# Delta-rule attention with an MLP on one core: a pair of chunks solved in whole blocks of 32, the accumulators' copies put ahead of two activations, pieces of the first pair moved

## The chip, the cores and the metric

The kernel runs on one core of a Trainium2 chip. A core has engines that run side by side, each with its own in-order queue: TensorE (PE, matmuls from SBUF into PSUM), VectorE (DVE), ScalarE (ACT), GpSimd (POOL) and SyncE (SP), which here only issues transfers (DMA). The metric is the device time of one execution in microseconds (us). Before the change it is 641.29 us, the median of 3 runs (641.17 to 642.59).

## The reference, cut to what matters

Four batches, 8 heads, 768 time steps, head size 48. Each head runs a delta rule over time, and the result, 3072 tokens of 384 features, goes through an MLP with 2048 hidden units.

```python
k_n = k / (norm(k) + 1e-06)
for t in range(768):
    y[t] = q[t] @ state
    v_old = k_n[t] @ state
    state = state + beta[t] * outer(k_n[t], v[t] - v_old)
h = y @ w_in
g = where(h >= 1, h, where(h <= -1, 0, (h + 1) ** 2 / 4))
out = g @ w_out
```

## The kernel before, in words

**Chunks.** Time is cut into 12 chunks of 64 steps, taken in 6 pairs. Within a chunk the recursion is replaced by a triangular system: keys against keys (gram_k, L193), the inverse of a unit triangular matrix of size 64 for each head and batch, and products with values, queries and the state. The state lies in SU. For one chunk g the pieces on PE are gram_k, gram_q (L206, queries against keys), chain_r (L390, the state's part is taken from the values), chain_u (L405), chain_y (L419, the output of the attention) and chain_d (L465, the state's update).

**The triangular inverse.** lanes (L253) copies the blocks of 32 on the diagonal, transposes them so that each of 128 lanes of DVE holds one block, and works out the norms of the keys, N, and the factor gm from beta. Then there are two ways:

- In halves (G < WHOLE): the two blocks of 16 of each block of 32 are inverted by solve (L293), 15 steps of a product and a subtraction on DVE. unlanes (L326) puts them back. merge16_a and merge16_b (L340, L352) join two blocks of 16 into one of 32 by matmuls on PE, once for each of the two chunks; their results are subtracted and transposed again on DVE (L361, L362).
- Whole (G >= WHOLE): lanes scales the block (L280), POOL cuts the triangle (L281, affine_select) and sets the diagonal, and solve_whole (L304) inverts the block of 32 in 30 steps (L310 product, L312 addition). unlanes_whole (L315) scales, transposes back, and makes the transposed copies (L318, L320, L323).

In both ways merge32 (L366) joins blocks of 32 into 64 on PE. WHOLE is 2 before the change: the first two pairs go in halves, the other four whole. (G in lanes counts pairs of chunks.)

**The MLP and its slots.** The main loop (L738) walks over 104 items. An item is one block of 128 hidden units for one pair of chunks, and the pairs are the stages G = 0 to 5. Stage 0 has 24 items, of which the first 8 and the last 8 cover only one chunk (256 columns), and the others have 16 items of 512 columns. For an item n, PE does up (L605, 9 matmuls into the accumulator "h", 2 buffers); ACT and DVE work out g from it in place (L735 twice, L754, then the max with h, L762); in the next item ACT and DVE split it in two parts, ghi and glo (L730, L731); and down (L614) of that item follows two items later (LAG), into four accumulators o0 to o3 that stay open for a stage. When the last block of a chunk is through, store (L628) copies the accumulators out, those with even number on ACT, those with odd number on DVE (L631), and sends them off over SP.

**How the attention is fitted in.** Each item has two half slots. plan(G) (L649) writes by hand which attention piece runs in which half slot while stage G of the MLP runs: at(pe, G, t, ...) puts a piece on PE at item t of the stage, at(fill, G, t, ...) steps of DVE work or loads. Slot t of an integer comes after up and before down of the item, and its results are moved out within the item; slot t + 0.5 comes after down, and its results are moved out at the start of the next item. During stage 0 the chunks 2 and 3 are made ready, during stage 1 the chunks 4 and 5, and so on; the first up of stage G + 1 needs the chain_y of its second chunk, whose rows are partly sent through SP (L460). All these PE pieces share two PSUM accumulators, named "ch": a piece can start only when the piece that held its accumulator before has been moved out.

In stage 0 DVE and ACT also unpack the MLP's weights, which arrive as 64-bit numbers (weight, L163; run(wu, ...) in the loop).

Of the kernel before, what the change touches and what calls it, by code (L numbers as in the profile page):

```python
# [23 lines left out]
SMALL = 20  # L24
SOON = 8
PASSES = ((0, 0), (0, 1), (1, 0))
WHOLE = 2
LAG = 2


# [1 line left out]
def delta_rule_moe(ctx: ExitStack, tc: tile.TileContext, kqa, kqb, kv, beta, w, out):  # L32
# [220 lines left out]
    def lanes(G):  # L253

        A = S["A"] = sb.tile([P, 32, 32], F32, name="A", bufs=1)
        if G < WHOLE:
            X = S["X"] = sb.tile([P, 2, 16, 16], F32, name="X", bufs=1)
            Xf = X.rearrange("l s c t -> l (s c t)")
            nc.gpsimd.memset(X, 0.0)
            for s in range(2):  # L260
                nc.gpsimd.memset(Xf[:, 256 * s:256 * s + 256:17], 1.0)
            nc.gpsimd.memset(ZT[:, :, :, 16:32], 0.0)
        for g in range(2):
            for r in (0, C):
                (nc.scalar.copy if G else nc.vector.tensor_copy)(out=GG[r:r + 32, g, :, 32:64], in_=GG[r:r + 32, g, :, 0:32])
            yield
        nc.vector.transpose(out=A, in_=GG[:, :, :, 32:64].rearrange("p g u t -> p t (g u)"))  # L267
        yield
        n = sb.tile([P, 32], F32, name="N2")
        nc.vector.tensor_copy(out=n, in_=A.rearrange("l j t -> l (j t)")[:, 0:1024:33])  # L270
        r = norms(n)
        N = S["N"] = sb.tile([P, 32], F32, name="N3")
        nc.vector.transpose(out=N, in_=n)
        gm = S["gm"] = sb.tile([P, 32], F32, name="gm")
        nc.vector.reciprocal(out=r, in_=n)
        nc.vector.tensor_tensor(out=gm, in0=r, in1=beta_sb[:, G, :], op=ALU.mult)
        nc.vector.tensor_tensor(out=gm, in0=gm, in1=r, op=ALU.mult)
        yield
        if G >= WHOLE:
            nc.vector.scalar_tensor_tensor(out=A, in0=A, scalar=-1.0, in1=gm[:, :, None].broadcast_to([P, 32, 32]), op0=ALU.mult, op1=ALU.mult)  # L280
            nc.gpsimd.affine_select(out=A, in_=A, pattern=[[-1, 32], [1, 32]], base=0, channel_multiplier=0,  # L281
                                    compare_op=ALU.is_gt, fill=0.0)
            nc.gpsimd.memset(A.rearrange("l c t -> l (c t)")[:, 0:1024:33], 1.0)
            return
        A16 = S["A16"] = sb.tile([P, 2, 16, 16], F32, name="A16", bufs=1)
        for s in range(2):
            b = slice(16 * s, 16 * s + 16)
            nc.vector.tensor_tensor(out=A16[:, s], in0=A[:, b, b], in1=gm[:, b, None].broadcast_to([P, 16, 16]), op=ALU.mult)
        X32 = S["X32"] = sb.tile([P, 32, 32], F32, name="A", bufs=1)
        nc.gpsimd.memset(X32, 0.0)  # L290
        yield

    def solve():  # L293

        X, A16 = S["X"], S["A16"]
        for j in range(15):
            n, m = j + 1, 15 - j
            pr = sb.tile([P, 240], F32, name="pr", bufs=1)[:, 0:2 * n * m].rearrange("l (s c t) -> l s c t", s=2, t=m)
            nc.vector.tensor_tensor(out=pr, in0=X[:, :, 0:n, j:j + 1].broadcast_to([P, 2, n, m]),
                                    in1=A16[:, :, j:j + 1, j + 1:16].broadcast_to([P, 2, n, m]), op=ALU.mult)  # L300
            nc.vector.tensor_tensor(out=X[:, :, 0:n, j + 1:16], in0=X[:, :, 0:n, j + 1:16], in1=pr, op=ALU.subtract)
            yield
# [23 lines left out]
    def unlanes():  # L326

        X, X32, gm = S["X"], S["X32"], S["gm"]
        for s in range(2):
            b = slice(16 * s, 16 * s + 16)  # L330
            nc.vector.tensor_tensor(out=X32[:, b, b], in0=X[:, s], in1=gm[:, None, b].broadcast_to([P, 16, 16]), op=ALU.mult)
        yield
        nc.vector.transpose(out=XT[:, :, :, 32:64].rearrange("p g u t -> p t (g u)"), in_=X32.rearrange("l c t -> l t c"))
        yield
        nc.vector.transpose(out=ZT[:, :, :, 0:16].rearrange("p g u c -> p c (g u)"), in_=X32[:, 0:16, :])
        yield
# [160 lines left out]
    def products(*pieces):  # L497
        return [p() for p in pieces]
# [145 lines left out]
    def chain(G, t, a):  # L644
        for j, f, g in ((0, chain_u, a), (0.5, chain_y, a), (1.5, chain_d, a), (2.5, chain_r, a + 1), (3.5, chain_u, a + 1), (4, chain_y, a + 1), (5, chain_d, a + 1)):
            if (f, g) != (chain_d, ntot - 1):
                at(pe, G, t + j, lambda f=f, g=g: f(g))

    def plan(G):  # L649

        a, b = 2 * G + 2, 2 * G + 3
        if G == NS - 1:
            return
        va, vb = scale_v(a), scale_v(b)
        if G == 0:
            ln, so, un = lanes(1), solve(), unlanes()
            at(pe, G, 0, lambda: chain_y(1))
            at(fill, G, 0.5, (load_q, 3))
            at(pe, G, 0.5, lambda: chain_d(1))
            at(pe, G, 1, lambda: place_beta(1, NS))  # L660
            at(fill, G, 1, (load_kv, 3))
            at(pe, G, 1.5, lambda: gram_k(a))
            at(pe, G, 2.5, lambda: gram_k(b))
            lane_steps(G, 7, ln)
            for j in range(8):
                at(fill, G, 9.5 + j / 2, (so, 2))
            at(pe, G, 11.5, lambda: gram_q(a))
            at(pe, G, 12.5, lambda: gram_q(b))
            at(fill, G, 13.5, (un, 1))
            at(fill, G, 13.5, (un, 9))  # L670
            for j in range(2):
                at(fill, G, 10 + j, (va, 1))
                at(fill, G, 16 + j, (vb, 1))
            at(pe, G, 13.5, lambda: chain_r(a))
            M = 14
            for j, f in enumerate((merge16_a, merge16_b)):
                for g in range(2):
                    at(pe, G, M + j + g / 2, lambda f=f, g=g: f(g))
            M = 16
            last = 24  # L680
        else:
            so, un = solves.pop(G)
            at(fill, G, 0.5, (va, 1))
            at(fill, G, 1, (va, 1))
            at(pe, G, 2.5, lambda: chain_r(a))
            at(pe, G, 4.5, lambda: gram_q(a))
            at(pe, G, 6, lambda: gram_q(b))
            cost, hs = 0, 0
            for j in range(1, 31):
                at(fill, G, (-0.5 if G == 1 else -1.5) + hs / 2, (so, 1))  # L690
                cost += j * (31 - j) + 150
                hs = int(cost / 9461 * (15 if G == 1 else 17))
            for j, t in enumerate((7, 7.5, 8, 8)):
                at(fill, G, t, (un, 1))
            at(fill, G, 9, (vb, 1))
            at(fill, G, 9.5, (vb, 1))
            M = 8.5
            last = 16
        for j, x in ((0, (0, None)), (0.5, (1, 0)), (2.5, (None, 1))):
            at(pe, G, M + j, lambda x=x: merge32(*x))  # L700
        chain(G, M + 1.5, a)
        if G < NS - 2:
            at(fill, G, 6.5 if G else 14, (load_k, a + 2))
            at(fill, G, M + 0.5, (load_k, b + 2, (nc.sync, nc.sync), True))
            at(pe, G, M + 1, lambda: gram_k(a + 2))
            at(pe, G, M + 3.5, lambda: gram_k(b + 2))
            lane_steps(G, M + 2, lanes(G + 2), 2.5, 3, 3.5, 4)
            solves[G + 1] = solve_whole(), unlanes_whole()
            at(fill, G, M + 3, (load_q, a + 2))
            at(fill, G, M + 5, (load_k, b + 2))  # L710
            at(fill, G, M + 6.5, (load_q, b + 2))
            at(fill, G, last + 0.5, (load_kv, a + 2))
            at(fill, G, last + 1.5, (load_kv, b + 2))
# [24 lines left out]
    for n, item in enumerate(items):  # L738
        at_, c = 2 * n, cols(item[2])
        finish(late)  # L740
        if last:
            rest(*last)
            ready.append(last[0])
        h = up(*item)

        s = sb.tile([P, 2 * NB], F32, name="s", bufs=2)
        relu(s[:, c], h[:, c], mid, -0.5)
        evicts = products(*pe.pop(at_, []))
        run(wu, 3 if n < 3 else 1)
        fills(at_)  # L750
        finish(evicts)
        run(wu, 1)
        relu(s[:, c], s[:, c], one, -1.0)
        nc.scalar.activation(out=s[:, c], in_=s[:, c], func=AF.Square)  # L754
        if len(ready) == LAG:
            x = ready.pop(0)
            down(*x)
            for b in x[2]:
                if left[x[0], b] == 0:
                    store(x[0], b)  # L760
        late = products(*pe.pop(at_ + 1, []))
        nc.vector.tensor_tensor(out=s[:, c], in0=h[:, c], in1=s[:, c], op=ALU.max)  # L762
        run(wu, 2)
        fills(at_ + 1)
        last = item, s
# [53 lines left out]
```

## Time and profile before

| | |
|---|---|
| median of 3 runs | 641.29 us |
| the profiled execution | 640.05 us |
| its span, first to last instruction | 638.3 us |
| PE busy | 596.0 us (93%) |
| DVE busy | 413.8 us (65%) |
| ACT busy | 389.9 us (61%) |
| POOL busy | 29.7 us (5%) |
| mean granted PE clock | 0.954 |

How to read the rows. A row of the grouped view gives the line of the kernel, the engine, the operation, what it writes and reads, the shape and the count; after the first bar the busy time of the group and the mean duration of one in ns; after the second bar the time that the engine idled just before them, and what ended that. A row of the timeline has the start, the duration, the engine and line, the operation, and in brackets the idle time before it with its releaser. In the view by stretches each engine has its busy time and, in brackets, its count of instructions. PE counts each fp32 matmul of a piece twice. An engine's busy time can be the time in which several small matmuls overlap. Items can be told by up: the nine matmuls of L610.

### The profile page before, as it was taken

To read this page: it belongs to the slowest core of one execution; us is meant where nothing else is said; L and a number is where in the kernel's file an instruction comes from. 1 tells how busy PE (TensorE), PEld (TensorE's weight loads), DVE (VectorE), ACT (ScalarE), POOL (GpSimd) and SP (SyncE) were. 2 spreads that over 40 slices of the span, in tenths; PEclk is the share of its full clock that TensorE was granted. 3 is DMA by queue.
4 is the path that set the end of the run, shared out by engine and by line. 5 is a ranking of instruction groups with operands and counts; after the bars stand their busy time and mean duration, and the time that the engine had idled before them with its cause. 6 is when DMAs were issued, how large, how long until landed. Compare 5 with 4: busy or idle time off the path is not lost.

```text
span 638.3 us, 21794 instructions
## 1 busy us (share of the span) xinstructions
PE 596.0 (93%) x9584; PEld 514.9 (81%) x9584; DVE 413.8 (65%) x862; ACT 389.9 (61%) x679; POOL 29.7 (5%) x62
## 2 busy tenths in 40 slices
PE   8977777898898899999999999999999999999996
PEld 7657676687887787888888888888888888899995
DVE  3869789894257895458993469973389954343332
ACT  4126477753875558775569665568646586566663
POOL 2003000000002000002000010000020000000000
PEclk8685579999999999999999999999999999999999
DMA  5933483002032411113401114310214100010002
GB/s 170 370 94 107 143 269 94 2 4 56 17 81 51 114 29 30 37 35 90 110 18 30 43 39 116 91 28 7 66 48 110 35 2 15 4 44 18 0 1 50
DMA packets 32431, 42.54 MB, mean 67 GB/s; under 512 B 7056, under 2 KB 27152, under 8 KB 32336
## 3 DMA queue, kind: packets, MB, share of 16 engines
q1 hardware_dynamic: 31200, 39.00, 21.5%
q10 hardware_dynamic: 880, 2.07, 1.0%
q8 instruction: 75, 1.23, 0.8%
q14 instruction: 20, 0.16, 0.1%
q0 software_dynamic: 256, 0.08, 0.1%
HBM read 34.05 MB, written 4.72 MB: 61 GB/s over the span
## 4 chain that ended last, share of the span: by engine, by line
PE 57%; DVE 21%; ACT 10%; issue 6%; DMA 3%; SPq 2%; POOL 1%; DVEq 0%; ACTq 0%
PE o L625 20%; PE h L610 18%; PE ch L553 4%; PE ch L430 3%; DVE glo L731 3%; DVE pr L310 3%; DVE A L312 2%; DVE s L762 2%; ACT s L735 2%; ACT GG L385 2%; PE ch L395 2%; ACT XT L387 2%; PE ch L375 2%; DVE SU L487 1%; DVE A L267 1%
## 5 line engine op out<-in xcount | busy, mean ns | idle before, releaser
L610 PE MATMUL h<-xb,wt 128*128 128x512 f32 (+1 forms) x936 | 226.1, 387 | 8.5 <-DVE s L762 5.8
L625 PE MATMUL o<-wt,ghi 128*128 128x384 f32 x768 | 200.9, 343 | 3.9 <-DVE wx L631 3.0
L610 PEld LDWEIGHTS h<-xb,wt 128*128 128x128 f32 x936 | 165.4, 191 | 41.6 <-DVE s L762 7.8
L625 PEld LDWEIGHTS o<-wt,ghi 128*128 128x128 f32 x768 | 137.2, 189 | 12.9 <-DVE wx L631 4.3
L762 DVE TENSOR_TENSOR s<-h,s 128x512 f32<-128x512 f32 (+1 forms) x104 | 66.9, 644 | 114.9 <-ACT s L754 114.8
L625 PE MATMUL o<-wt,glo 128*128 128x384 f32 x384 | 130.3, 339 | 0.6 <-DVE glo L731 0.5
L730 ACT CAST ghi<-s 128x512 fp32r<-128x512 f32 (+1 forms) x104 | 61.2, 589 | 106.7 <-DVE s L762 95.2
L735 ACT ACTIVATE s<-h,half 128x512 f32<-128x512 f32 (+1 forms) x104 | 68.0, 654 | 49.4 <-PE h L610 49.1
L731 DVE TENSOR_TENSOR glo<-s,ghi 128x512 fp32r<-128x512 f32 (+1 forms) x104 | 66.9, 643 | 43.3 <-ACT ghi L730 43.3
L625 PEld LDWEIGHTS o<-wt,glo 128*128 128x128 f32 x384 | 72.4, 189 | 2.3 <-DVE glo L731 2.3
L735 ACT ACTIVATE s<-s,one 128x512 f32<-128x512 f32 (+1 forms) x104 | 72.1, 693 | 2.6
L754 ACT ACTIVATE s<-s 128x512 f32<-128x512 f32 (+1 forms) x104 | 62.3, 599 | 3.3
L310 DVE TENSOR_TENSOR pr<-A 128x30 f32<-128x30 f32 (+14 forms) x120 | 39.3, 328 | 6.4 <-POOL A L281 4.5
L312 DVE TENSOR_TENSOR A<-A,pr 128x30 f32<-128x30 f32 (+14 forms) x120 | 39.8, 332 | 4.4
L430 PEld LDWEIGHTS ch<-Q,SU 64*64 64x64 f32 (+3 forms) x1056 | 23.7, 141 | 4.5 <-ACT ghi L730 1.5
L430 PE MATMUL ch<-Q,SU 64*64 64x64 f32 (+3 forms) x1056 | 26.0, 228 | 0.6 <-ACT SU L415 0.6
L553 PE MATMUL ch<-SU 128*128 128x64 f32 (+1 forms) x72 | 24.0, 521 | 0.0
L553 PEld LDWEIGHTS ch<-SU 128*128 128x128 f32 x72 | 15.2, 279 | 8.1 <-issue 8.0
L456 DVE TENSOR_TENSOR xb<-ch,xb 128x384 fp32r<-128x384 f32 x22 | 12.1, 551 | 14.5 <-ACT X L451 10.2
L226 DVE TENSOR_TENSOR Q<-ch,mask 64x512 f32<-64x512 f32 (+1 forms) x30 | 20.6, 687 | 0.4
L281 POOL TENSOR_SCALAR_AFFINE_SELECT A<-A 128x1024 f32<-128x1024 f32 x4 | 5.1, 1264 | 299.5 <-DMA xb<-X 261.1
L487 DVE TENSOR_TENSOR SU<-ch,SU 48x384 f32<-48x384 f32 (+1 forms) x30 | 16.6, 555 | 0.7 <-PE ch L472 0.3
(129 smaller groups left out, 605.7 us busy)
## 6 DMA issues: line engine op xcount, KB each, us to landing
wt<-in_w_dram SPq DMA_DIRECT2D x14, 768.0 KB, 7.4
out_dram<-wx SPq DMA_DIRECT2D x47, 96.0 KB, 2.2
KV<-in_kv_dram SPq DMA_DIRECT2D x36, 96.0 KB, 2.4
KV<-in_kv_dram SPq DMA_DIRECT2D x72, 48.0 KB, 2.3
KV<-in_kv_dram SPq DMA_DIRECT2D x12, 192.0 KB, 2.8
xb<-X SPq DMA_DIRECT2D x66, 32.0 KB, 2.1
K<-in_kqb_dram SPq DMA_DIRECT2D x12, 128.0 KB, 2.7
Q<-in_kqb_dram SPq DMA_DIRECT2D x12, 128.0 KB, 2.7
```

The lines of the kernel that those rows point to most:

```text
L310: nc.vector.tensor_tensor(out=pr, in0=A[:, 0:n, j:j + 1].broadcast_to([P, n, m]), in1=A[:, j:j + 1, j + 1:32].broadcast_to([P, n, m]), op= ...
L312: nc.vector.tensor_tensor(out=A[:, 0:n, j + 1:32], in0=A[:, 0:n, j + 1:32], in1=pr, op=ALU.add)
L430: nc.tensor.matmul(yy[i][o * C:o * C + C, e, p], SF[rows, u:u + C], w_[rows, x, k, :], **how)
L487: nc.vector.tensor_tensor(out=x, in0=y, in1=x, op=ALU.add)
L553: nc.tensor.matmul(idle[:, 0:m], SF[:, 0:P], SF[:, 0:m], start=True, stop=True)
L610: nc.tensor.matmul(h[:, cols(bs)], WT[f][:, 0, x, k * P:(k + 1) * P], XB[G][:, y, k, cols(bs)], start=(n == 0), stop=(n == 8))
L625: nc.tensor.matmul(oacc[G, k], (ghi, glo)[x][:, k * P:(k + 1) * P], WT[f][:, 1, y, :], start=(new and n == 0), stop=(left[G, b] == 0 and n ...
L730: nc.scalar.copy(out=ghi[:, c], in_=s[:, c])
L731: nc.vector.tensor_tensor(out=glo[:, c], in0=s[:, c], in1=ghi[:, c], op=ALU.subtract)
L735: nc.scalar.activation(out=out, in_=in_, func=AF.Relu, bias=bias, scale=scale)
L754: nc.scalar.activation(out=s[:, c], in_=s[:, c], func=AF.Square)
L762: nc.vector.tensor_tensor(out=s[:, c], in0=h[:, c], in1=s[:, c], op=ALU.max)
```

## The change

- **The second pair is inverted whole.** WHOLE goes from 2 to 1, and plan(0) uses solve_whole and unlanes_whole. The four merges of 16 leave PE. The steps are spread by a function that was a loop in plan before, over twelve half slots from item 9.
- **Other slots in stage 0.** chain_d(1) goes from 0.5 to 1, the placing of beta from 1 to 4, the key Grams from 1.5 and 2.5 to 2 and 3, the query Grams from 11.5 and 12.5 to 13 and 16, chain_r(2) from 13.5 to 14, the steps of unlanes from 13.5 to 15 to 16, the scaling of the second chunk's values from 16 and 17 to 17.5 and 18.5, the loads of values and keys half an item later. merge32, the chain and what hangs on them (M) move from 16 to 16.5.
- **The accumulators' copies.** In the loop, down and store now stand ahead of the second and third activation of the item. On PE nothing changes by that; on ACT the copies of store come before these activations.

```diff
-WHOLE = 2
+WHOLE = 1
...
+    def spread(G, t, n, so):
+        cost, hs = 0, 0
+        for j in range(1, 31):
+            at(fill, G, t + hs / 2, (so, 1))
+            cost += j * (31 - j) + 150
+            hs = int(cost / 9461 * n)
...
-            ln, so, un = lanes(1), solve(), unlanes()
+            ln, so, un = lanes(1), solve_whole(), unlanes_whole()
             at(pe, G, 0, lambda: chain_y(1))
             at(fill, G, 0.5, (load_q, 3))
-            at(pe, G, 0.5, lambda: chain_d(1))
-            at(pe, G, 1, lambda: place_beta(1, NS))
-            at(fill, G, 1, (load_kv, 3))
-            at(pe, G, 1.5, lambda: gram_k(a))
-            at(pe, G, 2.5, lambda: gram_k(b))
+            at(pe, G, 1, lambda: chain_d(1))
+            at(fill, G, 1.5, (load_kv, 3))
+            at(pe, G, 2, lambda: gram_k(a))
+            at(pe, G, 3, lambda: gram_k(b))
+            at(pe, G, 4, lambda: place_beta(1, NS))
             lane_steps(G, 7, ln)
-            for j in range(8):
-                at(fill, G, 9.5 + j / 2, (so, 2))
-            at(pe, G, 11.5, lambda: gram_q(a))
-            at(pe, G, 12.5, lambda: gram_q(b))
-            at(fill, G, 13.5, (un, 1))
-            at(fill, G, 13.5, (un, 9))
+            spread(G, 9, 12, so)
+            at(pe, G, 13, lambda: gram_q(a))
+            at(pe, G, 16, lambda: gram_q(b))
+            for t in (15, 15.5, 16, 16):
+                at(fill, G, t, (un, 1))
             for j in range(2):
                 at(fill, G, 10 + j, (va, 1))
-                at(fill, G, 16 + j, (vb, 1))
-            at(pe, G, 13.5, lambda: chain_r(a))
-            M = 14
-            for j, f in enumerate((merge16_a, merge16_b)):
-                for g in range(2):
-                    at(pe, G, M + j + g / 2, lambda f=f, g=g: f(g))
-            M = 16
+                at(fill, G, 17.5 + j, (vb, 1))
+            at(pe, G, 14, lambda: chain_r(a))
+            M = 16.5
...
-            at(fill, G, 6.5 if G else 14, (load_k, a + 2))
+            at(fill, G, 6.5 if G else 14.5, (load_k, a + 2))
...
-        relu(s[:, c], s[:, c], one, -1.0)
-        nc.scalar.activation(out=s[:, c], in_=s[:, c], func=AF.Square)
         if len(ready) == LAG:
             x = ready.pop(0)
             down(*x)
             for b in x[2]:
                 if left[x[0], b] == 0:
                     store(x[0], b)
+        relu(s[:, c], s[:, c], one, -1.0)
+        nc.scalar.activation(out=s[:, c], in_=s[:, c], func=AF.Square)
```

More of the change, by code (lines that the diff above doesn't have):

```diff
@@ L687, in plan @@
             at(pe, G, 6, lambda: gram_q(b))
[L688 to L692, printed above, removed]
+            spread(G, *((-0.5, 15) if G == 1 else (-1.5, 17)), so)
             for j, t in enumerate((7, 7.5, 8, 8)):
```

## The prediction

> **What bounds the kernel now.** I read the page first, then the busy time by stretches, then the timelines of TensorE (PE), VectorE (DVE) and the DMA issue queue (SP) through the first stage.
>
> ```profile
> span 638.3 us, 21794 instructions
> PE 596.0 (93%) x9584; PEld 514.9 (81%) x9584; DVE 413.8 (65%) x862; ACT 389.9 (61%) x679; POOL 29.7 (5%) x62
> ...
> PEclk8685579999999999999999999999999999999999
> ```
>
> Over the span PE is the bound. But the edit lies in the first stage (G=0, about 75 to 202 us), and there the stretches say something else:
>
> ```profile
> core 0: us, PE busy (x) PEld busy (x) DVE busy (x) ACT busy (x) POOL busy (x), PEclk, DMA share, GB/s
> 81.90:114.60 32.70, 25.25 (x302) 21.55 (x303) 32.41 (x52) 25.96 (x52) 0.00 (x0) 0.90 0.54 154
> 119.80:147.60 27.80, 24.46 (x403) 20.75 (x406) 26.38 (x69) 14.45 (x23) 0.96 (x1) 1.00 0.06 17
> 147.60:166.10 18.50, 17.52 (x663) 15.33 (x651) 5.67 (x11) 8.99 (x16) 2.08 (x4) 1.00 0.10 27
> 166.10:193.70 27.60, 26.08 (x722) 23.37 (x722) 11.41 (x25) 22.05 (x48) 0.00 (x0) 1.00 0.22 56
> ```
>
> From 81.9 to 114.6 DVE is busy 32.41 of 32.70 us (weight unpacking) and PE has 7.4 us free. From 119.8 to 147.6 DVE is busy 26.38 of 27.80 (the lane steps and the solve of the second pair). Only from 147.6 to 166.1 does DVE have room, 12.8 us, and there PE is full (17.52 of 18.50): that is where the four merges of 16 stand. So the stage is bound by DVE until 147 us and by PE from there. The question is what happens if DVE gets about as much work as that room holds.
>
> **The change, part by part. 1: D, beta and the key Grams.**
>
> ```profile
> 82.79 0.29 PE L472 MATMUL ch<-SU,KV 64*48 64x48 f32 x4 [1.62 <-DVE A L457]
> 89.42 1.16 PE L199 MATMUL ch<-K 48*64 48x64 f32 x62 [1.44 <-ACT beta_sb L135]
> ...
> 108.71 1.33 PE L610 MATMUL h<-xb,wt 128*128 128x256 f32 x9 [1.23 <-DVE s L762]
> ```
>
> Both waits come from pieces that follow each other into the two "ch" accumulators: chain_d(1) waits 1.62 us for those of chain_y(1), gram_k(2) waits 1.44 us for that of the beta placing. Moved apart, both waits can go, 3.1 us. But DVE is full behind them, and its instructions there are the same ones. PE then waits for DVE longer at the following items, as it does already in the third row (1.23 us). I take 0: the cover is the DVE queue. The bounds are a gain of 3.1 (DVE not the limit after all) and a loss of about 1 (ACT now waits inside the item for the Grams, and the weight casts queue behind that). The key and value loads that are issued half an item later keep their order on SP.
>
> **2: the solve.** This is the term that decides.
>
> ```profile
> L312 DVE TENSOR_TENSOR A<-A,pr 128x30 f32<-128x30 f32 (+14 forms) x120 | 39.8, 332 | 4.4
> L310 DVE TENSOR_TENSOR pr<-A 128x30 f32<-128x30 f32 (+14 forms) x120 | 39.3, 328 | 6.4 <-POOL A L281 4.5
> ...
> L301 DVE TENSOR_TENSOR X<-X,pr 128x30 f32<-128x30 f32 (+7 forms) x30 | 7.6, 255 | 1.0
> L299 DVE TENSOR_TENSOR pr<-X,A 128x30 f32<-128x30 f32 (+7 forms) x30 | 7.6, 252 | 0.8
> ...
> L323 DVE STREAM_TRANSPOSE GG<-XT 128x512 f32<-128x512 f32 x8 | 5.2, 685 | 0.0
> ...
> L318 DVE TENSOR_TENSOR A<-A,gm 128x1024 f32<-128x1024 f32 x4 | 4.9, 1217 | 0.0
> ...
> L362 DVE STREAM_TRANSPOSE GG<-XT 128x512 f32<-128x512 f32 x4 | 2.8, 711 | 0.1
> ...
> L335 DVE STREAM_TRANSPOSE XT<-A 128x512 f32<-128x512 f32 x2 | 2.0, 998 | 0.0
> ...
> L331 DVE TENSOR_TENSOR A<-X,gm 128x256 f32<-128x256 f32 x4 | 1.5, 420 | 0.1
> ...
> L361 DVE TENSOR_TENSOR XT<-XT,ch 128x256 f32<-128x256 f32 x2 | 0.8, 420 | 4.1 <-PE ch L356 4.1
> ```
>
> Thirty steps over whole blocks cost (39.3 + 39.8)/4 = 19.8 us of DVE in each later stage, fifteen over halves (7.6 + 7.6)/2 = 7.6: +12.2. The final scaling becomes one instruction of 1024 elements for two of 256, 1.22 - 0.84 = +0.4; the first scaling, in the same shapes, +0.4 again. The first step now waits for the triangle that POOL cuts: 4.5 us over 3 stages in the L310 row, so +1.5 of idle DVE, since nothing stands between the two here. One transpose goes (-1.0), two of 512 columns come (+1.4), the subtractions and transposes of the merges go (-0.8, -1.4). Sum: **+12.7 us on DVE**, nearly all of it ahead of the room at 147.6.
>
> Between 119.8 (max(8)) and 166.1 (end of max(16)) DVE has 26.4 + 5.7 = 32.1 us of work, so it gets 44.8 in 46.3. The full stretch holds 1.4 us of gaps in 27.8; left at that the sum is 46.2, carried over in proportion 47.2. Half a microsecond of value scaling leaves the stretch. So max(16) ends between 165.5 and 166.6: I take 166.1, the time of before, only that DVE now arrives there without a pause. The up-products keep step with it, each waiting for the "h" buffer that the max two items earlier frees.
>
> **3: what PE saves, and what it waits for.**
>
> ```profile
> L344 PE MATMUL ch<-XT,GG 32*32 32x16 f32 x256 | 2.7, 180 | 2.3 <-DVE KV L401 2.2
> ...
> L356 PE MATMUL ch<-A,XT 32*32 32x16 f32 x256 | 2.9, 180 | 0.2 <-issue 0.2
> ```
>
> ```profile
> 164.41 0.21 PE L373 MATMUL ch<-XT,GG 32*32 32x32 f32 x1
> ...
> 166.00 1.34 PE L610 MATMUL h<-xb,wt 128*128 128x256 f32 x9
> ...
> 178.12 1.20 PE L375 MATMUL ch<-GG 32*32 32x32 f32 x64 [0.37 <-DVE X L457]
> ...
> 165.70 0.42 DVE L762 TENSOR_TENSOR s<-h,s 128x256 f32<-128x256 f32 x1 [4.30 <-ACT s L754]
> L226 DVE TENSOR_TENSOR Q<-ch,mask 64x512 f32<-64x512 f32 (+1 forms) x30 | 20.6, 687 | 0.4
> ```
>
> PE is spared 2.7 + 2.9 = 5.6 us of merges and the 2.3 us waited ahead of them. It can't cash them in before 166, because DVE leads. Then the new order bites: merge32 of the first group needs a "ch" accumulator, gram_q(3) now stands directly ahead of it and holds both, and the masks that empty them (three of 0.69) lie on DVE behind the transposes of the solve, just ahead of max(16). Their first accumulator comes free one mask and one half-width max before the end: 166.1 - 0.7 - 0.4 = 165.0. Before, PE had at 166.0 both merge32 pieces done.
>
> Left for PE until the last chain_y of the stage ends: the work of 166.1 to 193.7 (26.1 us), one merge32 (1.2), the double one (164.41 to 166.00, 1.6) and one up of 256 columns that now stands ahead of chain_y(3) (1.3): 30.2 us. Its waits were 27.6 - 26.1 = 1.5; with Grams and merges closer together on two accumulators I put them at 3.0, twice that, with 1.5 and 4.5 as ends. 165.0 + 33.2 = 198.2 against 193.7: **+4.5**.
>
> **4: the border to the next stage.**
>
> ```profile
> 174.27 2.24 PE L430 MATMUL ch<-Q,SU 112*64 112x64 f32 x96
> 191.48 2.24 PE L430 MATMUL ch<-Q,SU 112*64 112x64 f32 x96
> 201.86 2.34 PE L610 MATMUL h<-xb,wt 128*128 128x512 f32 x9 [1.26 <-DVE A L312]
> 214.19 0.62 PE L625 MATMUL o<-wt,ghi 128*128 128x384 f32 x2 [1.77 <-DVE wx L631]
> ...
> 178.70 4.27 SPq L460 DMA_DIRECT2D xb<-X  x6
> 197.08 4.47 SPq L460 DMA_DIRECT2D xb<-X  x6
> ```
>
> The first up of stage 1 waits for the copies that the last chain_y sends over SP (the engine named, DVE L312, has no part in it). From the end of chain_y (193.7) to their issue took 3.4 us, after the earlier chain_y only 2.2 (176.5 to 178.7): in the first case the norms of the next pair stood ahead on DVE. The up that now goes first gives these norms time, so -1.1. Everything behind (queries, values, the accumulator copies at 214.19) hangs on SP's queue and shifts with it. **+4.5 - 1.1 = +3.4.**
>
> **5: accumulators copied out first.**
>
> ```profile
> 303.33 0.62 PE L625 MATMUL o<-wt,ghi 128*128 128x384 f32 x2 [0.42 <-ACT wx L631]
> ...
> 304.54 0.61 PE L625 MATMUL o<-wt,ghi 128*128 128x384 f32 x2 [0.42 <-DVE wx L631]
> ```
>
> ACT's copies move ahead of two activations; behind them wait these two, then max on DVE, then the cast of the next item, and none is due within an item. PE's first wait goes, but the second accumulator is copied by DVE, whose queue is not changed: PE waits until 304.54 as before. 0; the ends are -0.4 at each of two such borders and +0.4 if an activation comes late.
>
> The later stages are full on PE and untouched. Sum: 0 + 3.4 + 0. The profiled execution took 640.05 us, 1.75 beyond its span; it should become 643.5, the span 641.7. The median of the runs is 641.29, so the forecast is **644.7**.
>
> **The rivals.** A difference under 0.3% (1.9 us) can't be told from none.
>
> *PE leads after all* (faster). If DVE catches up before gram_q(3), by a solve that fits between the other work, the merges are pure saving: -5.6 - 2.3, and +1.3 for the up ahead of chain_y(3), -6.6: 634.7. For it speaks PE's 93%; against it that DVE is at 95% where the solve is put. It decides from 5 us less DVE work than I count. Chance 0.13.
>
> *Everything folds* (within 0.3%). Waits stay at 1.5 and the norms give back 1.1: 165.0 + 31.7 - 193.7 - 1.1 = +1.9, less up to 0.8 from part 5: 642.4. Chance 0.2. That the change doesn't do what it says can be excluded by reading: the constant sends lanes(1) into the branch for whole blocks, and the plan hands the same pair solve_whole.
>
> *The clock drops* (slower by more). PE gets new pauses of some 3 us; the longest shown at full clock is near 2.3 (row L344).
>
> ```profile
> 75.41 2.29 PE L610 MATMUL h<-xb,wt 128*128 128x256 f32 x9 [0.92 <-ACT SU L415]
> ```
>
> At the lower granted clock (0.5 in this slice) an up of 256 columns took 2.29 instead of 1.34. If the clock fell in the pause ahead of merge32, the merges, up(17) and as many microseconds again, some 6 us, would take 1.7 times as long: +4.3, 649.0. Chance 0.07. The Trainium skill (TensorE: Matmul & The Clock Gate, "Part 1: The HAM clock gate") has the PE fall to half rate after an idle window of about 3.4 us and come back after one busy window; by that the price would be one window, about +1.4, and 646.1. No row here shows a fall from full clock after such a pause.
>
> **How the numbers follow.** The forecast has 0.6, the rivals 0.13, 0.2 and 0.07. The range runs from 640.0 (the gain of part 1 would take 3.1 off the forecast, and waits of 1.5 another 1.5) to 648.0 (waits of 4.5, DVE at its upper end, a clock window). Within the forecast's own case about a tenth lies below +1.9. So faster 0.13, same 0.2 + 0.06 = 0.26, slower 0.54 + 0.07 = 0.61.
>
> **What would show it.** Right: DVE full from 119 to 166 with one idle of about 1.5 us behind the triangle; up waiting for max in items 11 to 16; merge32 starting near 165, with DVE L226 as releaser; the last chain_y of the stage ending near 198, and the first 512-column up of stage 1 near 205; stages 1 to 5 as long as before. Wrong: merge32 starting before 162 (then DVE was cheaper than summed), or the first up of stage 1 before 202. If PE's waits of 0.42 at the borders sink together with the stage lengths, part 5 was mis-costed.

## The result and the profile after

The changed kernel takes 645.3 us (median of 17 runs) where the kernel before takes 641.59 (17 runs beside them): a ratio of 1.0052 [1.0032, 1.0073], 3.7 us slower. One of the 17 runs of the changed kernel took 1088.3 us and is left out of the ratio. The forecast was +3.4 and 644.7. The profiled execution took 643.39 us, its span 641.7; both were forecast within 0.1 us (643.5, 641.7), and as shown below that is partly luck.

The page of the changed kernel, with the rows that answer those of before:

```profile
span 641.7 us, 20792 instructions
...
PE 590.3 (92%) x9072; PEld 511.4 (80%) x9072; DVE 423.9 (66%) x887; ACT 388.4 (61%) x677; POOL 29.3 (5%) x59
...
PEclk9775689989898999999999999999999999999999
```

PE has 5.7 us less to do and DVE 10.1 us more, and yet the span is longer by 3.4 us. The clock row, 9 without a break before from the seventh slice on, now dips to 8 in the ninth, eleventh and thirteenth. The busy time in the same stretches as before:

```profile
core 0: us, PE busy (x) PEld busy (x) DVE busy (x) ACT busy (x) POOL busy (x), PEclk, DMA share, GB/s
81.90:114.60 32.70, 23.85 (x295) 20.15 (x295) 31.12 (x49) 25.92 (x52) 0.00 (x0) 0.95 0.50 145
119.80:147.60 27.80, 22.69 (x155) 19.07 (x153) 24.88 (x66) 12.14 (x19) 3.49 (x6) 0.88 0.00 1
147.60:166.10 18.50, 14.93 (x251) 13.84 (x252) 16.27 (x34) 8.15 (x14) 0.00 (x0) 0.95 0.18 48
166.10:193.70 27.60, 25.87 (x753) 22.92 (x752) 9.09 (x21) 21.76 (x47) 0.00 (x0) 0.97 0.20 54
```

The room of DVE from 147.6 to 166.1 is filled (16.27 us busy where it had 5.67), and there PE, which was full before (17.52), now has 3.6 us free. The limit has moved from PE to DVE in that stretch, as forecast. DVE's timeline through the second pair's solve, from the first scaling to the max of item 16:

```profile
121.95 1.22 DVE L280 SCALAR_TENSOR_TENSOR A<-A,gm 128x1024 f32<-128x1024 f32 x1
124.60 0.19 DVE L310 TENSOR_TENSOR pr<-A 128x30 f32<-128x30 f32 x1 [1.43 <-POOL A L281]
...
160.77 1.31 DVE L323 STREAM_TRANSPOSE GG<-XT 128x512 f32<-128x512 f32 x2
161.99 2.08 DVE L226 TENSOR_TENSOR Q<-ch,mask 64x512 f32<-64x512 f32 x3
163.98 0.41 DVE L760 TENSOR_TENSOR s<-h,s 128x256 f32<-128x256 f32 x1
```

Between 124.60 and the end at 164.39 no row of DVE carries a bracket: it waits for nobody. The one wait, 1.43 us for the triangle from POOL, is the one forecast (1.5). Behind it the up of item 11 waits for a max on DVE (3.33 us), and the first merge32 waits for DVE's masks (3.06 us):

```profile
74.05 2.29 PE L610 MATMUL h<-xb,wt 128*128 128x256 f32 x9 [0.93 <-ACT SU L415]
...
127.42 4.21 PE L610 MATMUL h<-xb,wt 128*128 128x512 f32 x9 [3.33 <-DVE s L760]
...
163.49 1.48 PE L373 MATMUL ch<-XT,GG 32*32 32x32 f32 x64 [3.06 <-DVE Q L226]
164.90 2.29 PE L610 MATMUL h<-xb,wt 128*128 128x256 f32 x9
...
194.78 2.28 PE L430 MATMUL ch<-Q,SU 112*64 112x64 f32 x96
205.62 3.66 PE L610 MATMUL h<-xb,wt 128*128 128x512 f32 x9 [2.65 <-DVE pr L310]
```

The first up of stage 0 began at 74.05 here and at 75.41 before. The change alters nothing ahead of it, and in profiles of kernels with the same set-up it began anywhere from 74.05 to 76.60. So times are counted from this first up. The first merge32 starts 89.44 us after it (before 84.88, forecast 89.6); the last chain_y of the stage ends at 123.0 (before 118.3, forecast 122.8); the first up of stage 1 starts at 131.57 (before 126.45, forecast 129.85); the program ends at 567.7 (before 562.9, forecast 566.3). The forecast of the stage held within 0.2 us up to chain_y, missed the border by 1.7, and the early set-up of this execution gave 1.4 back.

One sign of the prediction did not come: of the ups of items 11 to 16 only the first waits for a max. The other waits for DVE stand ahead of chain_r(2) (1.48 and 0.35 us) and of merge32 (3.06 us), which need an accumulator that the masks on DVE have to empty.

### The profile page after: what moved, and what is told of

Read it like the earlier page. It is cut to its first block, busy times and chain, and to the rows that moved or that the text cites. A ratio compares the mean times of both kernels' runs of the same rounds, so it can differ in the third digit from the quotient of the medians.

```text
span 641.7 us, 20792 instructions
## 1 busy us (share of the span) xinstructions
PE 590.3 (92%) x9072; PEld 511.4 (80%) x9072; DVE 423.9 (66%) x887; ACT 388.4 (61%) x677; POOL 29.3 (5%) x59
## 4 chain that ended last, share of the span: by engine, by line
PE 56%; DVE 23%; ACT 12%; issue 6%; POOL 1%; DMA 1%; DVEq 0%; POOLq 0%; ACTq 0%; SPq 0%
PE o L625 19%; PE h L610 19%; PE ch L553 4%; DVE pr L310 4%; DVE glo L729 3%; DVE A L312 3%; PE ch L430 3%; ACT s L733 2%; DVE s L760 2%; ACT XT L387 2%; ACT GG L385 2%; PE ch L375 2%; PE ch L395 2%; DVE SU L487 1%; PE ch L212 1%
## 5 line engine op out<-in xcount | busy, mean ns | idle before, releaser
L610 PE MATMUL h<-xb,wt 128*128 128x512 f32 (+1 forms) x936 | 228.2, 389 | 13.5 <-DVE s L760 9.1
L610 PEld LDWEIGHTS h<-xb,wt 128*128 128x128 f32 x936 | 167.6, 193 | 47.4 <-DVE s L760 11.7
L760 DVE TENSOR_TENSOR s<-h,s 128x512 f32<-128x512 f32 (+1 forms) x104 | 67.0, 644 | 122.8 <-ACT s L758 122.8
L310 DVE TENSOR_TENSOR pr<-A 128x30 f32<-128x30 f32 (+9 forms) x150 | 49.2, 328 | 8.8 <-POOL A L281 6.3
L312 DVE TENSOR_TENSOR A<-A,pr 128x30 f32<-128x30 f32 (+9 forms) x150 | 49.8, 332 | 5.5
L226 DVE TENSOR_TENSOR Q<-ch,mask 64x512 f32<-64x512 f32 (+1 forms) x30 | 20.6, 686 | 0.4
L385 ACT ACTIVATE GG<-ch 32x512 f32<-32x512 f32 x20 | 11.8, 589 | 9.4 <-PE ch L373 9.2
```

The costliest lines, as they stand in the source:

```text
L310: nc.vector.tensor_tensor(out=pr, in0=A[:, 0:n, j:j + 1].broadcast_to([P, n, m]), in1=A[:, j:j + 1, j + 1:32].broadcast_to([P, n, m]), op= ...
L312: nc.vector.tensor_tensor(out=A[:, 0:n, j + 1:32], in0=A[:, 0:n, j + 1:32], in1=pr, op=ALU.add)
L385: nc.scalar.mul(out=GG[r:r + 32, ga, :, 0:32], in_=y1[r:r + 32], mul=-1.0)
L610: nc.tensor.matmul(h[:, cols(bs)], WT[f][:, 0, x, k * P:(k + 1) * P], XB[G][:, y, k, cols(bs)], start=(n == 0), stop=(n == 8))
```

## The experiments

All ratios are against the kernel before, run beside them on the same chip. The changed kernel itself (645.3 us) ran only in the first comparison. The kernel before had medians of 640.8 to 641.7 us in all four, so differences of 1 us between medians of different comparisons say nothing.

### The three parts one by one

**copies_only**: the kernel before, with the copies ahead of the two activations.

```diff
-        relu(s[:, c], s[:, c], one, -1.0)
-        nc.scalar.activation(out=s[:, c], in_=s[:, c], func=AF.Square)
         if len(ready) == LAG:
...
+        relu(s[:, c], s[:, c], one, -1.0)
+        nc.scalar.activation(out=s[:, c], in_=s[:, c], func=AF.Square)
```

> The kernel before with one edit: down and store ahead of the second and third activation of an item. By the theory (DVE sets the stage, the solve costs): no change, 641.6 within 1 us; at the borders of stages 2 and 3 the wait of 0.42 us for the accumulator copied by ACT goes and the wait for the one copied by DVE grows by as much. Rival, the copies give something at each border: 0.8 to 2 us faster. Rival, held-up activations cost: 1 us slower or more, with PE waiting for max in the items behind a store.

641.16 against 640.8 us, 1.0000 [0.998, 1.0021]. PE's waits for the copied accumulators from 200 us on (us in total, times, longest), first before, then copies_only:

```profile
PE o L625 <- DVE wx L631: 3.0, 4, 1.8
...
PE o L625 <- ACT wx L631: 0.9, 2, 0.4
```

```profile
PE o L625 <- DVE wx L631: 3.9, 4, 1.3
```

ACT's 0.9 us are gone, and DVE's are 0.9 us more: PE waits as long as before, for the other engine. Part 5 is worth nothing, for the reason forecast.

**moves_only**: the kernel before, with D, beta and the key Grams in their new slots.

```diff
-            at(pe, G, 0.5, lambda: chain_d(1))
-            at(pe, G, 1, lambda: place_beta(1, NS))
-            at(fill, G, 1, (load_kv, 3))
-            at(pe, G, 1.5, lambda: gram_k(a))
-            at(pe, G, 2.5, lambda: gram_k(b))
+            at(pe, G, 1, lambda: chain_d(1))
+            at(fill, G, 1.5, (load_kv, 3))
+            at(pe, G, 2, lambda: gram_k(a))
+            at(pe, G, 3, lambda: gram_k(b))
+            at(pe, G, 4, lambda: place_beta(1, NS))
```

> The kernel before with one edit: chain_d(1), the placing of beta, the key Grams and the loads in the slots of the change. By the theory: no change, 641.6 within 1 us; the waits of 1.62 and 1.44 us in front of chain_d(1) and gram_k(2) go, and one of about 3 us comes in front of gram_k(2), for the additions of chain_d(1) on DVE. Rival, PE sets this stretch: 3 us faster.

641.38 against 640.8 us, 1.0006 [0.9984, 1.0027]. The two waits of before (1.62 and 1.44 us) became shorter or vanished, and a longer one came in front of the first key Gram, which now follows chain_d(1) directly. Its row from the waits of 74 to 118 us in moves_only:

```profile
PE ch L199 <- DVE SU L487: 3.8, 1, 3.8
```

Two waits exchanged for one that is longer, and no time lost or gained (the first merge32 starts 84.93 us after the first up, before 84.88): PE is not what bounds this stretch.

**solve_only**: the changed kernel with the early pieces and the copies as they were before.

```diff
-            at(pe, G, 1, lambda: chain_d(1))
...
-            at(pe, G, 4, lambda: place_beta(1, NS))
+            at(pe, G, 0.5, lambda: chain_d(1))
+            at(pe, G, 1, lambda: place_beta(1, NS))
...
+        relu(s[:, c], s[:, c], one, -1.0)
+        nc.scalar.activation(out=s[:, c], in_=s[:, c], func=AF.Square)
         if len(ready) == LAG:
```

> The changed kernel with the early pieces and the order of copies and activations as before; what is left is the whole solve and the later slots that belong to it. By the theory the whole difference sits here: 645.3 within 1 us, merge32 starting some 89 us after the first up, the last chain_y of stage 0 ending some 123 us after it. Rival, the sum is made of three parts: below 643.5 here.

644.92 against 640.8 us, 1.0059 [1.0038, 1.008]: the whole difference of the changed kernel. Of the three parts only the solve matters.

### Less and more work on DVE

**half_steps**: the changed kernel, where solve_whole leaves out its odd steps, 15 of 30, in stage 0 only. The inverse of that pair is therefore not worked out. The slots stay.

```diff
+            if j % every:
+                yield
+                continue
...
-            ln, so, un = lanes(1), solve_whole(), unlanes_whole()
+            ln, so, un = lanes(1), solve_whole(2), unlanes_whole()
```

> The changed kernel, in which stage 0 leaves out the even half of the thirty... that is every second step of the whole solve, so that the inverse of this pair is not worked out; slots, pieces and order are the same. It takes about 10 us from DVE. By the theory (DVE is full until the query Gram of chunk 3, and PE waits for it) the time falls by most of that until PE is full: to between 636 and 639. Rival, the order decides (the Gram directly ahead of merge32 on two accumulators, PE's own work): 644 or more. Rival, the granted clock alone makes the loss: about 643, the pauses of 3 us gone.

639.08 against 640.8 us, 0.997 [0.9946, 0.9995], and 5.8 us faster than solve_only beside it, at the upper edge of what was expected. DVE's busy time over the span fell by 8.8 us (423.9 in the changed kernel, 415.1 here). The first merge32 in its profile:

```profile
160.14 1.69 PE L376 MATMUL ch<-XT,GG 32*32 32x32 f32 x64 [1.73 <-DVE Q L226]
```

The first up began at 75.88, so this is 84.3 us after it (changed kernel 89.4, before 84.9), and the last chain_y of the stage ends at 118.6 (123.0, 118.3): the delay is gone. The profiled execution took 643.42 us, 4.3 more than the median. It loses behind the stage: the clock falls for 6.83 us at 215.1, and stage 1 lasts 93.0 us, where it lasts 89.6 in the changed kernel.

**more_dve**: the changed kernel with 20 products of 240 elements more on DVE, whose results nobody uses, spread over items 10 to 14.5.

```diff
+            ex = extra(20)
+            for j in range(10):
+                at(fill, G, 10 + j / 2, (ex, 2))
```

> The changed kernel with twenty additional DVE products of 240 elements (0.41 us each, about 8.5 us with the gaps), two in each half slot from item 10 to 14.5 of stage 0; their result is not used. By the theory (DVE has no free time there and PE waits for it) nearly all of it shows: 7 to 9 us slower than the changed kernel, some 653. Rival, PE or the order of its pieces sets the stage: within 2 us of 645.

653.72 against 641.37 us, 1.0182 [1.0153, 1.0211]. The added work (its group in the trace) and the merge32 behind it:

```profile
L660 DVE TENSOR_TENSOR pr<-A 128x240 f32<-128x240 f32 x20 | 8.2, 408 | 0.6
```

```profile
173.49 1.92 PE L373 MATMUL ch<-XT,GG 32*32 32x32 f32 x64 [4.03 <-DVE Q L226]
```

8.2 us of work and 0.6 of gaps make the kernel 8.4 us slower than the changed one (653.72 - 645.3): nearly each microsecond on DVE is a microsecond of time. Downwards 8.8 us of work brought 5.8 us. By both, DVE's load bounds the stage in the changed kernel. That the way down gave less than the way up fits a stage in which PE takes over before all 8.8 us are gone, but no run shows that point itself.

### Order, the clock and the border

**gram_early**: the changed kernel with gram_q(3) at 14.5 instead of 16, so that its masks no longer stand directly ahead of merge32.

```diff
-            at(pe, G, 16, lambda: gram_q(b))
+            at(pe, G, 14.5, lambda: gram_q(b))
```

> The changed kernel with the query Gram of chunk 3 at slot 14.5 instead of 16, so that its masks stand on DVE ahead of the scaling and the transposes of the solve, and its two accumulators are free long before merge32. By the theory (DVE full) merge32 then waits for the transposes, which come 2 us later: it starts about 1 us earlier, and the time falls by 0 to 1.5 us, to 644 to 645. Rival, the order is the cost (the Gram directly ahead of merge32): 3 us or more faster, 642 or less.

644.53 against 641.67 us, 1.0038 [1.002, 1.0057], within what was expected. The loss is not resolvably smaller than that of the changed kernel (1.0052 [1.0032, 1.0073]). That fits masks that are work for DVE wherever they stand.

**pauses_filled**: the changed kernel with 16 and 14 matmuls of 384 columns whose result nobody uses, in PE's pauses ahead of the first merge32 and ahead of the first up of stage 1.

```diff
+            at(pe, G, 16.5, lambda: keep(16))
+            at(pe, G, 23.5, lambda: keep(14))
```

> The changed kernel with additional matmuls in the pauses of PE ahead of the first merge32 (16 of 384 columns) and ahead of the first up of stage 1 (14), into an accumulator whose content is not used. If the granted clock falls because PE pauses, the ups behind these pauses take 1.33 and 2.34 us instead of 2.29 and 3.66, and the time falls by 1 to 2.5 us. If it does not, or the work added is in the way: 0 to 2 us slower.

646.21 against 641.67 us, 1.0067 [1.0042, 1.0092]. What it did to the clock shows in stretches of 3.4 us, one ahead of each of the two places. In the changed kernel (the first and third row), each with the stretch that follows it:

```profile
160.80:164.20 3.40, 0.71 (x45) 0.74 (x47) 3.35 (x7) 0.00 (x0) 0.00 (x0) 1.00 0.41 119
164.20:167.60 3.40, 3.40 (x77) 3.11 (x73) 0.19 (x1) 2.51 (x5) 0.00 (x0) 0.50 0.04 11
201.80:205.20 3.40, 1.17 (x6) 0.85 (x6) 3.22 (x11) 1.22 (x3) 2.87 (x5) 0.99 0.18 39
205.20:208.60 3.40, 2.98 (x7) 2.43 (x8) 2.37 (x9) 0.00 (x0) 0.63 (x2) 0.51 0.43 115
```

In pauses_filled, the stretch ahead of each, and then its timeline:

```profile
160.80:164.20 3.40, 3.10 (x19) 2.81 (x19) 3.36 (x7) 0.04 (x1) 0.00 (x0) 1.00 0.35 96
201.80:205.20 3.40, 3.40 (x20) 3.40 (x21) 3.22 (x11) 1.26 (x3) 2.83 (x5) 1.00 0.23 52
```

```profile
164.19 1.20 PE L373 MATMUL ch<-XT,GG 32*32 32x32 f32 x64 [0.30 <-DVE Q L226]
165.32 1.33 PE L610 MATMUL h<-xb,wt 128*128 128x256 f32 x9
...
205.32 2.26 PE L610 MATMUL h<-xb,wt 128*128 128x512 f32 x9
...
216.92 0.62 PE L625 MATMUL o<-wt,ghi 128*128 128x384 f32 x2 [0.95 <-DVE wx L631]
```

PE was busy for 0.71 and 1.17 us of the 3.4, and the granted clock of the next 3.4 us was 0.50 and 0.51. With the pauses filled it stayed full, and the ups took 1.33 and 2.26 us instead of 2.29 and 3.66. So the falls of the clock at these two places come from the pauses.

Whether filling them gains time is not shown. By the medians it did not (646.21 us, the changed kernel 645.3), against the 1 to 2.5 us that were expected. In the profiles, counted from the first up, the last chain_y ends 0.7 us and the program 1.0 us earlier than in the changed kernel, although the accumulators are waited for again (0.95 us). But this profiled execution is the fastest of its 12 (643.13 us, mean clock 0.956; the two runs of 646.21 us had 0.951 and 0.947), and the added matmuls may be in the way at the border, where the up follows them without a pause.

**before_two_queues** and **after_two_queues**: the kernel before, and the changed kernel, with three of the six transfers of the last chain_y of stage 0 issued by POOL.

```diff
-                        nc.sync.dma_start(out=xb.bitcast(F32)[r + D:r + C, :, k, g % 2 * NB:g % 2 * NB + NB],
+                        (nc.gpsimd if g == 3 and r else nc.sync).dma_start(out=xb.bitcast(F32)[r + D:r + C, :, k, g % 2 * NB:g % 2 * NB + NB],
```

> The same edit in the kernel before. By the theory of the border its idle of 1.26 us in front of the first up of stage 1 goes, and of the 1.77 us in front of the third accumulator a part: 1 to 3 us faster than before, 638 to 640. Rival: within 0.5 us of before.

> The changed kernel, in which three of the six copies of the last chain_y of stage 0 are issued by POOL instead of SP. By the theory of the border (the first up of stage 1 waits for the fourth copy on SP, and queries, values and accumulator copies hang behind it) the idle of 2.65 us in front of that up goes, and the time falls by 1.5 to 4 us, to 641 to 643.5. Rival, the values of chunk 4 or DVE set the border anyway: within 1 us of 645.

Before: 639.33 against 641.67 us, 0.9958 [0.9938, 0.9978], faster. In its profile the first up of stage 1 waits for nothing and starts 6.7 us after chain_y ends (8.1 before); that execution took 642.32 us, 3.0 above the median, and has the fall of the clock shown in the last section. Changed: 645.43, 1.0045 [1.0024, 1.0065], no gain that can be resolved, and the expected one did not come. In its timeline a part of the pause ahead of the first up of stage 1 is left, and the wait for the accumulators is back:

```profile
207.78 2.34 PE L610 MATMUL h<-xb,wt 128*128 128x512 f32 x9 [1.14 <-DMA xb<-X]
...
218.65 0.61 PE L625 MATMUL o<-wt,ghi 128*128 128x384 f32 x2 [0.67 <-DVE wx L631]
```

**norms_later**: the changed kernel with the norms of the next pair (and the first scaling) half an item later in stage 0, behind chain_y's subtractions on DVE.

```diff
-            lane_steps(G, M + 2, lanes(G + 2), 2.5, 3, 3.5, 4)
+            lane_steps(G, M + 2, lanes(G + 2), *((2.5, 3, 3.5, 4) if G else (2.5, 3, 4, 4.5)))
```

> The changed kernel with the norms of the pair after next and the step behind them half an item later in stage 0, so that they stand behind the last chain_y's subtractions on DVE. The prediction took 1.1 us off for this, which the changed kernel didn't show. If the norms are what holds the copies up, their issue comes 2.2 us after chain_y instead of 3.4, the first up of stage 1 about 1.1 us earlier, and the time falls by 0 to 1.2 us (644 to 645). If something else does: the same 3.4 us and no change.

643.27 against 641.37 us, 1.0021 [1.0000, 1.0042], by the medians 2.0 us less than the changed kernel, where at most 1.2 were expected; the intervals of the two ratios overlap. The border in norms_later, on PE and then on SP's queue:

```profile
197.21 2.28 PE L430 MATMUL ch<-Q,SU 112*64 112x64 f32 x96
...
205.86 2.33 PE L610 MATMUL h<-xb,wt 128*128 128x512 f32 x9 [1.72 <-DVE glo L729]
```

```profile
201.69 3.87 SPq L460 DMA_DIRECT2D xb<-X  x6
```

From the end of chain_y (199.49) to the issue it takes 2.2 us, the figure that the prediction wanted here, and to the first up of stage 1 6.4 us (8.6 in the changed kernel).

### A version that beats both

**before_values_first**: the kernel before, with two queues, and in stage 0 the loads of the next values ahead of those of the next queries.

```diff
-            at(fill, G, last + 0.5, (load_kv, a + 2))
+            at(fill, G, last + 0.5 if G else M + 6, (load_kv, a + 2))
```

**after_all**: the changed kernel with the same, and with gram_early and norms_later.

```diff
-            at(pe, G, 16, lambda: gram_q(b))
+            at(pe, G, 14.5, lambda: gram_q(b))
...
-            lane_steps(G, M + 2, lanes(G + 2), 2.5, 3, 3.5, 4)
+            lane_steps(G, M + 2, lanes(G + 2), *((2.5, 3, 3.5, 4) if G else (2.5, 3, 4, 4.5)))
...
-            at(fill, G, last + 0.5, (load_kv, a + 2))
+            at(fill, G, last + 0.5 if G else M + 6, (load_kv, a + 2))
```

> The kernel before with the last chain_y's copies issued by SP and POOL, and with the values of chunk 4 loaded ahead of the queries of chunk 5. By the theory of the border the rest of the waits there (the copy of the third accumulator behind the values on DVE) goes: another 0.3 to 1 us, 1.5 to 3.5 us faster than before. Rival, nothing further: as with the two queues alone, ratio 0.996.

> The changed kernel with all edits that could help it: the query Gram of chunk 3 at 14.5, the norms half an item later, the copies issued by SP and POOL, the values of chunk 4 ahead of the queries. By the theory DVE's load stays, so that it gains the border's part alone, 2 to 4 us: 641 to 643, and stays behind the kernel before with the same two edits at the border. Rival, order and border make the whole loss: below 640.

before_values_first: 637.77 against 641.37 us, 0.9934 [0.991, 0.9959], the fastest kernel of the study. after_all: 642.51, 1.0006 [0.9988, 1.0024]. SP's queue in before_values_first, and then PE:

```profile
196.32 2.65 SPq L460 DMA_DIRECT2D xb<-X  x3
199.01 0.59 SPq L98 DMA_DIRECT2D KV<-in_kv_dram  x1
```

```profile
199.68 2.26 PE L610 MATMUL h<-xb,wt 128*128 128x512 f32 x9
...
209.96 0.63 PE L625 MATMUL o<-wt,ghi 128*128 128x384 f32 x2 [0.16 <-DVE wx L631]
```

The first up of stage 1 now waits for nothing (1.26 us before), and the accumulators for 0.16 us (1.77 before). With the same two edits at the border in both, and two more in its favour, the changed kernel is still 4.7 us behind the one with halves. Its border is not free of waits, though. PE in after_all:

```profile
205.93 2.36 PE L610 MATMUL h<-xb,wt 128*128 128x512 f32 x9 [0.52 <-DVE s L760]
210.18 2.38 PE L610 MATMUL h<-xb,wt 128*128 128x512 f32 x9 [0.84 <-DVE s L760]
...
215.06 0.62 PE L625 MATMUL o<-wt,ghi 128*128 128x384 f32 x2 [0.94 <-DVE wx L631]
```

Counted from the first up, its last chain_y of stage 0 ends 2.8 us later than in before_values_first, its first up of stage 1 starts 0.8 us later, and its program ends 3.0 us later. So a part of the delay up to chain_y remains, the border takes most of it up, and the waits behind it (2.3 us, all for DVE, against 0.16) bring it back. How much of that is the solve and how much the norms that were put behind chain_y was not separated.

## Why the prediction was right, and where it was not

**Step 1 (early moves, 0): right** in the time: the waits changed their place (moves_only). The place was not the forecast one. The ups of this stretch wait no longer than before (4.6 us for max against 5.1), and the new wait stands ahead of the first key Gram.

**Step 2 (the solve, +12.7 us on DVE): right in sum, with its items a little off.** The groups of the steps after:

```profile
L310 DVE TENSOR_TENSOR pr<-A 128x30 f32<-128x30 f32 (+9 forms) x150 | 49.2, 328 | 8.8 <-POOL A L281 6.3
L312 DVE TENSOR_TENSOR A<-A,pr 128x30 f32<-128x30 f32 (+9 forms) x150 | 49.8, 332 | 5.5
```

They grew by 9.9 and 10.0 us for a forecast of 19.8. In all DVE's busy time grew by 10.1 us, where 11.2 were summed; but the gaps between dependent instructions, which I let grow hardly or in proportion, took about what that saved. max(16) ended 90.3 us after the first up (164.39 - 74.05), for a forecast of 90.7 (166.1 - 75.41).

**Step 3 (merge32 at 165.0, chain_y +4.5): right in the mechanism, and in the sum by luck.** The releaser is DVE L226, as named. From merge32 to the end of chain_y it took 33.57 us for a forecast of 33.2, but with other terms: PE was busy for 31.70 us instead of 30.2, since the clock stood at half for 3.41 us of it, and waited 1.87 us instead of 3.0. With the clock full (pauses_filled) it was 30.60 and 2.30. So the work was summed rightly, the waits were put too high, and the clock, counted as nothing, filled the gap. Three later profiles of kernels with gram_q(3) and the solve in the same places (solve_only, after_two_queues, norms_later) had merge32 at 91.2 to 91.5 instead of 89.4, a fourth (pauses_filled) at 89.4, probably for the reason told below, so the agreement within 0.2 us holds for this execution and not for each.

**Step 4 (the border, -1.1): failed.** I let the up that now goes first give the norms time to pass. But the plan hangs the norms on the same M as chain_y, so they moved half an item too and stayed ahead. DVE at the border in the changed kernel, and SP behind it:

```profile
198.93 0.19 DVE L277 TENSOR_TENSOR gm<-gm,r 128x32 f32<-128x32 f32 x1
199.04 0.55 DVE L456 TENSOR_TENSOR xb<-ch,xb 128x384 fp32r<-128x384 f32 x1
```

```profile
200.51 4.79 SPq L460 DMA_DIRECT2D xb<-X  x6
```

From the end of chain_y (197.06) to the issue it took 3.45 us, as before (3.4), and not 2.2. The first up of stage 1 waited 2.65 us and then ran 3.66 us at the low clock. Part of this came back: the wait of 1.77 us for the copied accumulators, which I let shift along, does not occur after the change. norms_later shows that the mechanism was real and its order misread: with the norms moved, the 2.2 us appear.

**Step 5 (copies, 0): right**, as copies_only shows.

**The rivals.** *PE leads after all* is refuted by more_dve. *Everything folds* did not come, though after_all comes close to it with other edits. *The clock drops* came in part, and the forecast counted nothing for it. The prediction said that no row shows a fall after a pause of some 3 us. It passed over two falls of the kernel before, 3.41 us each at 84.0 and 90.9, behind the waits of 1.62 and 1.44 us of its part 1 (its stretch from 81.90 to 114.60 has a clock of 0.90). In the changed kernel rows show falls after 3.33 us (an up of 4.21 instead of 2.24), 3.06 (2.29 instead of 1.33) and 2.65 us (3.66 instead of 2.34). The Trainium skill (TensorE: Matmul & The Clock Gate, "Part 1: The HAM clock gate") puts the fall behind an idle window of about 3.4 us and the return behind one busy window; the trace agrees with the length at the two places above (3.4 us). The fall after 3.33 us lasted two such steps (6.8 us), and the clock fell also where PE was idle for less than a window; there the measurement decides. Another pause, ahead of chain_r(2), differs between profiles. First norms_later, then the changed kernel's own profile:

```profile
149.50 0.42 PE L395 MATMUL ch<-SU,K 48*64 48x48 f32 x2 [2.65 <-DVE Q L226]
150.13 1.95 PE L395 MATMUL ch<-SU,K 48*64 48x48 f32 x62 [0.22 <-DVE Q L226]
```

```profile
147.76 0.28 PE L395 MATMUL ch<-SU,K 48*64 48x48 f32 x2 [1.48 <-DVE Q L226]
148.39 1.14 PE L395 MATMUL ch<-SU,K 48*64 48x48 f32 x62 [0.35 <-DVE Q L226]
```

In the first the clock falls here for 6.8 us and merge32 comes 1.7 us later. In the eight profiles with the whole solve at full length the two falls go together: where the fall at item 11's up lasts 6.83 us there is none at chain_r(2) (the changed kernel, pauses_filled, after_all), and where it lasts 3.41 us there is one (solve_only, after_two_queues, norms_later, gram_early, more_dve).

Such falls go along with the spread of the times. Each run lists its mean granted clock: in the changed kernel three runs at 0.950 took 642.5 to 643.4 us, the profiled one among them, and the twelve at 0.940 to 0.945 took 644.2 to 646.8. The falls may also be a part of the loss. Runs of the kernel before with a clock of 0.949 to 0.951 have a mean of 641.3 us (23 runs), the three of the changed kernel 643.1, which is 1.8 us and not 3.7; but the mean clock of the changed kernel's runs is 0.945, and that of the kernel before 0.952. So the forecast of +3.4 may have come close in part because a lower clock, which it did not count, made up for something counted too high. This is a comparison of groups and not an experiment: no run filled the pause at chain_r(2), and the mean clock holds the set-up too.

## What to carry to other kernels

An engine with 65% of the span can still be the bound of the one stage that is changed: read the stretch, sum both engines there, and ask what the receiving engine's room is worth before moving work to it. When a piece is moved, list all that hangs on the same slot variable; what "now goes first" may have moved along. At a border between stages, a second issue queue for three transfers and an earlier place for one load were worth 3.6 us here, as much as the change lost.

## What was not expected of the hardware

- **The clock also falls without a long pause.** before_two_queues has no pause above 0.89 us near 170 us, and yet (stretches of 3.4 us):

```profile
167.00:170.40 3.40, 2.30 (x74) 1.80 (x61) 0.42 (x1) 2.57 (x6) 0.00 (x0) 1.00 0.00 0
170.40:173.80 3.40, 3.11 (x66) 3.00 (x67) 0.89 (x2) 3.31 (x8) 0.00 (x0) 0.53 0.02 5
```

  PE was busy for 2.30 of 3.40 us, much of it with matmuls of 32 columns, and the clock fell to half for 6.8 us.

  The records of the granted clock show an order in this. In all 14 profiles it changes only a whole number of steps of 3.41 us after its first change. From 70 us on, up to the last 12 us, each such step at full clock in which PE was busy for less than 1.6 us was followed by half the clock, and none with more than 2.6 us; in between both occur. So it counts whether a pause lies within one step or across two: in norms_later the step ahead of chain_r(2) had PE busy for 0.92 us, in the changed kernel the pause lies across two steps that had 2.59 and 2.40. What decides between 1.6 and 2.6 us stays open.
- **Issuing in a row took longer than one transfer.** Six transfers of 32 KB cost SP 4.47 us to issue one after the other, while each lands 2.1 us after its issue in the median. The Trainium skill (DMA: Bandwidth & Descriptors, "Issuing engines are not separate DMA queues") says that issuing from several engines saves only the issue time, usually small; here that time was the wait, and splitting it made the kernel before 2.3 us faster.
